# Loading one expert's second weight matrix whole instead of in column slabs, at the end of a soft-MoE kernel

## The chip, the cores and the metric

The kernel runs on one core of a Trainium2 chip. The metric is the device time of one execution in microseconds (us), lower is better. Every number below comes from the profiles, the traces or the timed runs of this kernel and its variants, except where the Trainium skill is named. Most executions of the kernel before agree within 0.3%. One run of the kernel before took 372.67 us and is left out wherever fast runs are compared.

In the profiles PE is TensorE's matmuls and PEld its weight loads, ACT is ScalarE, DVE is VectorE, POOL is GpSimd, SP is SyncE, which issues the stores. The granted clock (PEclk) is the share of TensorE's full clock that it was given. SBUF is the on-chip memory of tiles, PSUM the one in which the matmuls' sums lie, in parts called banks.

## The reference

Sliding-window and dilated attention (8 batches, 8 heads, 576 positions, 64 per head), followed by a soft mixture of experts (MoE). Only the second part matters here:

```python
logits = x @ phi                       # x: 4608 tokens x 512; phi: 512 x 32 slots
d = softmax(logits, axis=0)            # over tokens
slot_input = (d.T @ x).reshape(8, 4, 512)
for e in range(8):                     # w1[e]: 512 x 1024, w2[e]: 1024 x 512
    h = np.maximum(slot_input[e] @ w1[e], 0.0)
    slot_out[e] = h @ w2[e]            # 4 slots of each expert
out = softmax(logits, axis=1) @ slot_out.reshape(32, 512)   # 4608 x 512
```

No output row can be finished before all eight `w2` have arrived. But an output *column* needs only that column of every `w2`.

## The kernel before

A small list scheduler written in Python orders the instructions of all engines and adds the semaphore waits. Weights are read as 4-byte floats and written to SBUF as bf16 by DMAs issued from GpSimd, in one long stream behind q, k and v. The stream ends with `w2` of experts 6 and 7, and these two are loaded in two slabs of 256 columns: all of slab 0, then all of slab 1. While slab 1 is still coming in, the outputs of columns 0 to 255 are computed, and those of the first `NA = 2.5` groups of 512 tokens are stored by halves, in pieces of 256 KB. The other groups are stored with all 512 columns.

```python
wq += [w1_piece(e, 2 if e == 0 else 0) for e in range(8)]
wq += [w2_piece(e) for e in range(5)] + [w2_piece(5, 0, 4), w2_piece(5, 4, 4)]   # 5 in two halves by rows
for s in range(2):                                                               # 6 and 7 in slabs of columns
    wq += [w2_slab(6, s), w2_slab(7, s, 0, 4), w2_slab(7, s, 4, 2),
           w2_slab(7, s, 6, 1), w2_slab(7, s, 7, 1)]
# ... (cut)
l2((0, 1, 2, 3), 0, 0, 512)            # l2: the sum h @ w2 of these experts, rows 32*(e % 4) of a PSUM bank
l2((4,), 0, 0, 512)
for y in range(2):
    l2((5,), 0, 0, 512, range(4 * y, 4 * y + 4), [b_w5h[y]])
# SOx: ScalarE copies rows 0-63 (experts 0, 1, 4, 5: finished) to SBUF as bf16
# SOy: VectorE copies rows 64-127 (experts 2, 3) to SBUF as f32
for x in (1, 2):                       # column halves
    l2((6,), x, 256 * x - 256, 256, bufs=[b_w2[6][x - 1]])
    for y, cs in enumerate((range(4), range(4, 6), range(6, 7), range(7, 8))):
        l2((7,), x, 256 * x - 256, 256, cs, [b_w2h[y][x - 1]])
    # SO0, SO1: VectorE adds rows 64-127 of this bank (experts 6, 7) to the copy SOy
# ... (cut) output tiles of 128 tokens: one matmul, then ScalarE and VectorE in turn scale it into SBUF, then a store
```

PE waits at each `l2` until that piece of weights has landed (0.85 us before slab 0 of expert 6 in the trace below). And SO0 needs SOy, which needs everything summed into the bank before it.

The softmax here doesn't subtract the row's maximum and nothing guards it: scores larger than these inputs give would overflow.

## Time and profile before

| | before |
|---|---|
| median of the runs, us | 178.0 (3 runs), 177.87 (6 runs) |
| span of the profiled execution, us | 176.1 |
| last weight piece landed | 152.19 |
| first store issued | 148.57 |
| first store landed on all 16 engines | 152.90 |
| last store landed | 175.61 |

"Landed" is the last of the 16 semaphore increments of a transfer in the trace.

Four rows of the slice table of the profile page (kernel before). Each of the 40 digits is one slice of 4.4 us: busy share of PE in tenths, granted TensorE clock in tenths, busy share of the DMA engines, and GB/s written by them.

```profile
PE   0008786799698998999998989996779676797000
...
PEclk9999999789999999999999999999755999999955
DMA  5999999999999999999999999999999999999997
GB/s 186 233 210 210 224 201 210 227 201 209 220 210 208 219 214 208 214 217 205 216 215 204 209 216 221 220 212 216 216 220 203 204 195 196 296 312 415 422 419 318
```

DMA is busy all the time, so the time is that of the transfers: 61.9 MB read, then 9.44 MB stored. The table counts a load by what it writes as bf16, half of what it reads, so 216 GB/s there is some 430 GB/s of reading. The rise at slice 34 (from 149.7 us) is the first stores.

The transfers by issue (kernel before): KB as written, median us from issue to landing.

```profile
out_dram<-ar SPq DMA_DIRECT2D x6, 1024.0 KB, 8.6
...
ar<-in_moe_w_dram POOLq DMA_DIRECT2D x5, 512.0 KB, 28.1
out_dram<-ar SPq DMA_DIRECT2D x10, 256.0 KB, 3.8
```

The ten stores of 256 KB are the halves of two and a half groups.

The chain of waits that ended last, in order of time (kernel before): start, us, what.

```profile
120.13 32.05 DMA ar<-in_moe_w_dram
...
152.23 0.30 PE ps L857
...
152.55 0.44 DVE ar L881
...
153.04 0.42 PE ps L901 x2
```

From 120 to 152.19 us the chain is one wait for weights. After the last landing comes 0.3 us of matmul, one addition of 0.44 us, and outputs.

### The profile page before, as it was taken

What the parts mean: (1) busy time and instruction counts of PE and PEld (TensorE: products, weight loads), DVE (VectorE), ACT (ScalarE), POOL (GpSimd) and SP (SyncE); (2) the same over time, 40 slices, a digit from 0 to 9 for tenths busy, and PEclk for the clock granted to TensorE, in tenths of its full rate; (3) what the DMA queues carried; (4) which work ended last, traced back from release to release, by engine and by line L of the source; (5) the groups of instructions that cost most, each with busy time, mean ns of one, the idle gap of its engine ahead of it and who ended that gap; (6) DMA issues with size and microseconds to landing.
All of it is one profiled execution on the core that took longest, in us unless ns stands there. A gap on an engine that the chain in (4) does not pass through costs nothing.

```text
span 176.1 us, 4787 instructions
## 1 busy us (share of the span) xinstructions
PE 129.5 (74%) x2102; PEld 86.8 (49%) x2102; DVE 120.5 (68%) x218; ACT 104.4 (59%) x165; POOL 44.9 (25%) x90
## 2 busy tenths in 40 slices
PE   0008786799698998999998989996779676797000
PEld 0005564567566776676777567765434334431000
DVE  6899395669998989989998999657220014399200
ACT  2404378568879969889889788884301113299000
POOL 7659622214142223311460000394000000000000
PEclk9999999789999999999999999999755999999955
DMA  5999999999999999999999999999999999999997
GB/s 186 233 210 210 224 201 210 227 201 209 220 210 208 219 214 208 214 217 205 216 215 204 209 216 221 220 212 216 216 220 203 204 195 196 296 312 415 422 419 318
DMA packets 17492, 41.26 MB, mean 234 GB/s; under 512 B 1728, under 2 KB 8384, under 8 KB 15040
## 3 DMA queue, kind: packets, MB, share of 16 engines
q0 software_dynamic: 13328, 30.41, 90.2%
q1 hardware_dynamic: 4144, 10.55, 15.7%
q8 instruction: 16, 0.26, 0.5%
q14 instruction: 4, 0.03, 0.0%
HBM read 61.93 MB, written 9.44 MB: 405 GB/s over the span
## 4 chain that ended last, share of the span: by engine, by line
DMA 32%; PE 23%; DVE 21%; ACT 10%; POOL 4%; issue 2%; POOLq 0%; DVEq 0%
DMA ar<-in_moe_w_dram 18%; DMA ar<-in_v_dram 14%; PE ps L509 6%; DVE ar L488 6%; DVE ar L913 6%; ACT ar L548 5%; POOL ar L372 3%; PE ps L603 3%; PE ps L570 3%; ACT ar L670 2%; PE ps L693 2%; DVE ar L614 2%; PE ps L516 2%; PE ps L526 2%; ACT ar L576 2%
## 5 line engine op out<-in xcount | busy, mean ns | idle before, releaser
L548 ACT ACTIVATE ar<-ps 128x1152 bf16<-128x1152 f32 (+1 forms) x32 | 38.0, 1186 | 22.8 <-PE ps L533 13.2
L488 DVE STREAM_TRANSPOSE ar<-ar 128x576 uint32<-128x576 uint32 x40 | 48.3, 1239 | 0.6 <-DMA ar<-in_k_dram 0.3
L509 PE MATMUL ps<-ar 128*128 128x320 bf16 (+1 forms) x128 | 23.8, 312 | 15.5 <-DVE ar L488 13.7
L614 DVE TENSOR_TENSOR ar<-ps,fs 96x768 bf16<-96x768 f32 (+1 forms) x32 | 26.3, 822 | 1.2
L576 ACT ACTIVATE ar<-ps 128x768 bf16<-128x768 bf16 x32 | 25.0, 812 | 1.1 <-PE ps L570 1.0
L509 PEld LDWEIGHTS ps<-ar 128*128 128x128 bf16 x128 | 10.8, 102 | 21.0 <-DVE ar L488 13.7
L603 PE MATMUL ps<-ar 128*128 128x65 bf16 x320 | 15.6, 199 | 4.2 <-ACT ar L548 4.2
L570 PE MATMUL ps<-ar 128*128 128x128 bf16 x192 | 15.9, 229 | 1.8 <-DVE ar L614 1.0
L603 PEld LDWEIGHTS ps<-ar 128*128 128x128 bf16 x320 | 12.8, 101 | 7.4 <-ACT ar L548 4.8
L910 ACT ACTIVATE ar<-ps,fs 128x512 f32<-128x512 f32 (+1 forms) x23 | 11.4, 638 | 7.6 <-PE ps L901 7.6
L335 POOL DMA_DIRECT2D ar<-in_k_dram x16 | 8.9, 553 | 27.5 <-DVE ar L488 26.7
L610 DVE RECIPROCAL fs<-ps 96x12 f32<-96x12 f32 (+1 forms) x32 | 6.6, 206 | 12.7 <-PE ps L603 12.2
L570 PEld LDWEIGHTS ps<-ar 128*128 128x128 bf16 x192 | 12.4, 118 | 2.9 <-DVE ar L614 1.2
L913 DVE TENSOR_SCALAR ar<-ps,fs 128x512 f32<-128x512 f32 (+1 forms) x23 | 12.7, 629 | 1.0 <-PE ps L901 1.0
L335 POOL DMA_DIRECT2D ar<-in_v_dram x16 | 8.8, 547 | 13.7 <-DVE ar L488 10.4
L857 PE MATMUL ps<-ar 128*32 128x512 bf16 (+1 forms) x80 | 9.6, 338 | 2.9 <-DMA ar<-in_moe_w_dram 1.4
L693 PE MATMUL ps<-ar 128*128 128x288 bf16 x64 | 10.2, 307 | 1.2 <-ACT ar L677 1.2
L335 POOL DMA_DIRECT2D ar<-in_q_dram x16 | 8.7, 545 | 8.8 <-DVE fs L610 5.3
L901 PE MATMUL ps<-ar 128*128 128x512 bf16 (+1 forms) x46 | 9.9, 340 | 1.3 <-DVE ar L881 1.0
L670 ACT ACTIVATE ar<-ps 128x576 bf16<-128x576 bf16 x16 | 9.7, 659 | 0.9 <-PE ps L654 0.7
L673 ACT ACTIVATE ar<-ps 128x1024 bf16<-128x1024 bf16 x8 | 8.2, 1030 | 2.5 <-PE ps L660 2.3
L494 DVE STREAM_TRANSPOSE ar<-ar 128x160 uint32<-128x160 uint32 (+1 forms) x32 | 9.5, 409 | 0.1
(75 smaller groups left out, 182.8 us busy)
## 6 DMA issues: line engine op xcount, KB each, us to landing
ar<-in_moe_w_dram POOLq DMA_DIRECT2D x12, 1024.0 KB, 25.9
out_dram<-ar SPq DMA_DIRECT2D x6, 1024.0 KB, 8.6
ar<-in_k_dram POOLq DMA_DIRECT2D x16, 288.0 KB, 21.1
ar<-in_q_dram POOLq DMA_DIRECT2D x16, 288.0 KB, 21.5
ar<-in_v_dram POOLq DMA_DIRECT2D x16, 288.0 KB, 20.5
ar<-in_moe_w_dram POOLq DMA_DIRECT2D x5, 512.0 KB, 28.1
out_dram<-ar SPq DMA_DIRECT2D x10, 256.0 KB, 3.8
ar<-in_moe_w_dram SPq DMA_DIRECT2D x1, 1024.0 KB, 5.1
```

The costliest lines, as they stand in the source:

```text
L335: return pool.dma_start(a(o_stg + (s * 3 + j) * 1152, [[1, 1152]]), src[b, 4 * dl:4 * dl + 4].rearrange("h (p t) d -> (h p) (t d)", p=32))
L488: return dve.transpose(au(o_dst, [[1, 18], [18, 32]]), au(src, [[32, 18], [1, 32]]))
L509: pe.matmul(pf(h, 0, [[1, W]]), a(o_id, [[1, 128]]), a(msk, [[1, W]]), start=True, stop=False)
L548: eo = op(ACT, lambda P=P, W=W: act.activation(a(P, [[W, 4], [1, W]]), AP(ps, 0, [[4096, 128], [512, 4], [1, W]]), ACTF.Exp, scale=SCALE), ...
L570: last = pe.transpose(pb(bank.idx, bb * 256 + par * 32, [[64, 4], [1, 32]]), src, a(o_id, [[1, 128]]))
L576: op(ACT, lambda t=t, bank=bank: act.activation(a(o_vb[vs] + 3 * t * VBK, [[66, 12], [2, 32], [1, 2]]), pb(bank.idx, 0, [[64, 12], [1, 32] ...
L603: last = pe.matmul(pf(bank.idx + x, 65 * t, [[1, 65]]), w, a(VB + t * VBK + 66 * h, [[1, 65]]), start=True, stop=True)
L614: op(DVE, lambda hp=hp, bank=bank: dve.tensor_tensor(a(ox + 128 * hp, [[64, 2], [256, NT], [1, 64]], 0, rows), pf(bank.idx, 0, [[512, 2], ...
L670: fn = lambda c=c + x, bank=bank: act.activation(a(o_xt[xt] + 576 * c, [[1, 576]]), pb(bank.idx, 0, [[1, 576]]), ACTF.Copy)
L693: last = pe.matmul(pf(bank.idx, 0, [[1, 288]]), a(o_phis + 128 * c, [[1, 128]]), a(o_xt[xt] + 576 * c + 288 * g, [[1, 288]]), start=(c == ...
L910: op(ACT, lambda: act.activation(dst, src(), ACTF.Copy, scale=sca), actt(cw, .1), prio + .1, reads=[bank, b_rinv], writes=wr, name=f"OE{G} ...
L913: op(DVE, lambda: dve.tensor_scalar(dst, src(), sca, None, op0=AluOp.mult), dvet(cw, True) + .08, prio + .1, reads=[bank, b_rinv], writes= ...
```

## The change

Slabs of columns mean short packets: a slab is written in pieces of 512 B, a whole `w2` in pieces of 8 KB. The change keeps slabs for expert 7 alone, loads experts 5 and 6 whole, and stores two groups by halves instead of two and a half, since less of the stream is left to overlap with.

```diff
-    wq += [w2_piece(e) for e in range(5)] + [w2_piece(5, 0, 4), w2_piece(5, 4, 4)]
+    wq += [w2_piece(e) for e in range(7)]
     for s in range(2):
-        wq += [w2_slab(6, s), w2_slab(7, s, 0, 4), w2_slab(7, s, 4, 2),
+        wq += [w2_slab(7, s, 0, 4), w2_slab(7, s, 4, 2),
                w2_slab(7, s, 6, 1), w2_slab(7, s, 7, 1)]
# ... (cut: buffers, stop flags)
-    for y in range(2):
-        l2((5,), 0, 0, 512, range(4 * y, 4 * y + 4), [b_w5h[y]])
-    op(ACT, ... SOx: rows 0 to 63 ...)
-    op(DVE, ... SOy: rows 64 to 127 ...)
+    l2((5,), 0, 0, 512)
+    l2((6,), 0, 0, 512)
+    op(ACT, ... SOx: rows 0 to 95 ...)
+    op(DVE, ... SOy: rows 96 to 127 ...)
     for x in (1, 2):
-        l2((6,), x, 256 * x - 256, 256, bufs=[b_w2[6][x - 1]])
         for y, cs in enumerate((range(4), range(4, 6), range(6, 7), range(7, 8))):
             l2((7,), x, 256 * x - 256, 256, cs, [b_w2h[y][x - 1]])
-        op(DVE, ... SO0, SO1: rows 64 to 127 ...)
+        op(DVE, ... SO0, SO1: rows 96 to 127 ...)
-    NA = 2.5
+    NA = 2
```

Expert 6's sum, once two column halves behind their own slabs, becomes eight matmuls of 512 columns behind one landing, and SOx and SOy now come after them.

## The prediction

> **What bounds the kernel now.** The DMA engines, almost from end to end. The slice table has DMA at 9 tenths in every slice but the first and last, PE only 74% busy. In the chain of waits, the weight loads hold 120.1 to 152.2 us; evictions and stores follow. Two floors in a row: the load stream (61.9 MB read), whose last piece lands at 152.2 us (semaphore landings), and 9.44 MB of stores, last landed at 175.6 us.
>
> Packet records give the rates: whole-w2 loads (8 KB packets written) 429 GB/s of fp32 read; slabs of 256 columns (512 B packets) 388; half-width stores (1 KB rows) about 350, one 256 KB store every 0.75 us; full stores (8 KB) 420, 2.50 us per 1 MB. That short packets are slower agrees with the Trainium skill, "DMA: Bandwidth & Descriptors", section "Why small descriptors are slow". Loads and stores share the 16 engines (same page, "Issuing engines are not separate DMA queues"): from 149 to 152 us stores take 64, 172, 252 GB/s while slabs fall to 308, 198, 112. But the slabs are not delayed: their 2 MB took 5.43 us beside stores and 5.38 us without. Half of the engines finish each load some 2.3 us early, and the first stores fill these.
>
> **What changes, with costs (estimates from these durations).**
> 1. Expert 6's w2, 2.1 MB, at 429 instead of 388 GB/s: stream 0.5 us shorter, last landing 152.2 -> 151.7. Gain: 0.5 us. Expert 5 whole: nothing, 4 and 8 KB packets ran equally fast.
> 2. One half-width pair and a 512 KB store become part of a full store: 10 x 0.75 + 1.35 + 6 x 2.5 = 23.8 us becomes 8 x 0.75 + 7 x 2.5 = 23.5 us. Gain 0.3 us, partly hidden before in the early engines.
> 3. Loss: the first column half is complete later. After expert 5 came 5.4 us of slabs until 146.8 us; now 4.9 us (expert 6) + 2.7 us (expert 7's first slab): 149.0 us. The first store's issue moves from 148.6 to 150.8, its first bytes from 149.5 to 151.7 us, when the stream has ended on all engines: the early ones idle from 149.3, the late ones 0.3 us. The overlap is lost.
> 4. Expert 6's eight 512-column matmuls, 0.215 us each, finish at about 148.0 us, before the slabs need PE. The second half's first store can start its bytes 2.8 us after the last landing, at 154.5; four half stores cover 151.7 to 154.7. So no second hole, where before the early engines had one (258 and 187 GB/s at 153 to 155 us).
>
> **Sum.** First store lands at 152.8 to 152.9 (as before, 152.9), then 7 x 0.75 + 7 x 2.5 = 22.75 us: last landing about 175.6 us, against 175.6. The shorter stream pays for the stores' later start. Predicted time 177.9 us, 80% range 177.2 to 178.7. Faster by over 2%: 1%; within 2%: 97%; slower by over 2%: 2%.
>
> **What would show it.** (1) Last weight landing at 151.7, 0.5 us sooner. (2) First store issued near 150.8, with a dip in DMA in the slice at 149 to 152 us, and the dip at 153 to 155 gone. (3) 512 B packets halved, to 2048; 8 half stores. (4) All the same up to 136 us. (5) First store landed near 152.9, then stores back to back.
>
> **What would make it wrong.** A hole after the fourth half store (up to +0.7 us), if evictions or the last sum run late; a larger skew of the engines with 2 MB pieces; half stores at 0.68 us, as on the late engines before (-0.5 us).

## More of the kernel before

The clock is down in slices 28 to 30 (counted from 0), at half from 125.6 to 135.8 us in the trace, and full from there to 166 us.

The instructions between the end of expert 5 and the first store (timeline, kernel before): start, us, engine, line, what, and in brackets the idle time before and what ended it. L857 is `l2`, L872 and L875 are SOx and SOy, L881 is SO0, L901 the output matmuls.

```profile
143.27 0.59 ACT L872 ACTIVATE ar<-ps 64x512 bf16<-64x512 f32 x1 [5.84 <-PE ps L857]
143.27 0.69 DVE L875 COPY ar<-ps 64x512 f32<-64x512 f32 x1 [4.68 <-PE ps L857]
...
144.09 1.05 PE L857 MATMUL ps<-ar 128*32 128x256 bf16 x8 [0.85 <-DMA ar<-in_moe_w_dram]
...
145.47 1.61 PE L857 MATMUL ps<-ar 128*32 128x256 bf16 x8 [0.34 <-DMA ar<-in_moe_w_dram]
...
147.12 0.43 DVE L881 TENSOR_TENSOR ar<-ps,ar 64x256 bf16<-64x256 f32 x1 [3.16 <-PE ps L857]
...
147.61 1.29 PE L901 MATMUL ps<-ar 128*128 128x256 bf16 x10 [0.52 <-DVE ar L881]
147.94 1.93 ACT L910 ACTIVATE ar<-ps,fs 128x256 f32<-128x256 f32 x5 [4.08 <-PE ps L901]
...
148.57 2.86 SPq L922 DMA_DIRECT2D out_dram<-ar  x5
```

A group is shown with the shape of its first matmul, and a group of `l2` can hold several. The copies SOx and SOy are done at 143.96 us, long before slab 0 is complete at 146.76. What counts is therefore short: landing, the last matmul, SO0 at 147.12, output matmuls, evictions, first store issued at 148.57.

The same stretch by windows (kernel before): length in us, busy us of each engine with instruction counts, then granted clock, DMA share (the packets' times over the span of 16 engines, which comes out above 1 here), GB/s.

```profile
core 0: us, PE busy (x) PEld busy (x) DVE busy (x) ACT busy (x) POOL busy (x), PEclk, DMA share, GB/s
136.00:142.00 6.00, 4.67 (x68) 2.39 (x57) 0.36 (x2) 0.69 (x1) 0.00 (x0) 1.00 1.18 201
142.00:146.40 4.40, 3.18 (x22) 1.49 (x18) 0.69 (x1) 0.59 (x1) 0.00 (x0) 1.00 1.45 196
146.40:149.80 3.40, 2.20 (x16) 1.49 (x16) 2.17 (x6) 1.85 (x5) 0.00 (x0) 1.00 1.42 199
149.80:152.00 2.20, 1.90 (x14) 0.93 (x12) 0.31 (x1) 0.08 (x1) 0.00 (x0) 1.00 1.22 287
```

PE holds its full clock (1.00) all through.

## The result, and the profile after

The changed kernel ran at 179.46 us (median of 6, 178.84 to 180.1), outside the predicted 177.2 to 178.7. The ratio to before is 1.009, 95% interval 1.0066 to 1.0113. Ratios are the mean time of one kernel's fast runs over that of the other's of the same rounds, so they are not quite the ratio of the medians quoted. That is slower, but by less than 2%.

| | before | after | predicted |
|---|---|---|---|
| median, us | 177.87 | 179.46 | 177.9 |
| slab 0 landed | 146.76 | 149.11 | 149.0 |
| last weight landed | 152.19 | 151.82 | 151.7 |
| SOx and SOy start | 143.27 | 149.78 | not given; expert 6's sum ends at about 148.0 |
| first store issued | 148.57 | 152.08 | 150.8 |
| first store landed | 152.90 | 154.27 | 152.8 to 152.9 |
| last store landed | 175.61 | 177.18 | about 175.6 |

The slice table (kernel after; slices of 4.4 us):

```profile
PE   0009776799698999999999788995777457896000
...
PEclk9999999789999999999999999999999956999755
DMA  5999999999999999999999999999999999599997
GB/s 190 230 211 207 224 203 210 224 204 209 222 207 210 222 206 209 219 208 211 220 208 213 207 222 215 220 216 212 216 216 218 210 196 148 189 371 413 419 417 321
```

There is a DMA hole that was not there before: slices 33 and 34 (146.5 to 155.4 us) move 148 and 189 GB/s, against 196 and 296. And the clock row has moved: nothing at slices 28 to 30, but 5 and 6 in slices 32 and 33, just where expert 6 is summed.

The transfers by issue (kernel after):

```profile
ar<-in_moe_w_dram POOLq DMA_DIRECT2D x14, 1024.0 KB, 27.3
out_dram<-ar SPq DMA_DIRECT2D x7, 1024.0 KB, 8.6
...
out_dram<-ar SPq DMA_DIRECT2D x8, 256.0 KB, 2.8
```

The transfers are as intended.

The chain of waits (kernel after):

```profile
114.13 32.27 DMA ar<-in_moe_w_dram
...
146.44 3.31 PE ps L856 x12
...
149.78 0.71 DVE ar L874
...
150.58 0.44 DVE ar L879
...
151.15 0.40 PE ps L899 x2
...
151.57 1.66 DVE ar L911 x4
```

The chain no longer hangs on the last weights. It leaves the weights at 146.40 us, with expert 6's landing, and then runs through 3.31 us of matmuls, the copy SOy (0.71), the addition SO0 and the first evictions.

The timeline from expert 6's landing to the first store (kernel after; L856 is `l2`, L871 and L874 are SOx and SOy, L879 is SO0, L899 the output matmuls):

```profile
146.44 3.30 PE L856 MATMUL ps<-ar 128*32 128x512 bf16 x16 [2.15 <-DMA ar<-in_moe_w_dram]
...
149.78 0.59 ACT L871 ACTIVATE ar<-ps 96x512 bf16<-96x512 f32 x1 [15.35 <-PE ps L856]
149.78 0.70 DVE L874 COPY ar<-ps 32x512 f32<-32x512 f32 x1 [14.19 <-PE ps L856]
150.58 0.43 DVE L879 TENSOR_TENSOR ar<-ps,ar 32x256 bf16<-32x256 f32 x1
...
151.15 1.04 PE L899 MATMUL ps<-ar 128*128 128x256 bf16 x8 [1.41 <-DVE ar L879]
151.46 1.20 ACT L908 ACTIVATE ar<-ps,fs 128x256 f32<-128x256 f32 x3 [1.09 <-PE ps L899]
151.57 0.88 DVE L911 TENSOR_SCALAR ar<-ps,fs 128x256 f32<-128x256 f32 x2 [0.57 <-PE ps L899]
152.08 0.39 SPq L920 DMA_DIRECT2D out_dram<-ar  x1
```

The first line holds sixteen matmuls: the eight of expert 6 (512 columns, rows 64 to 95) and, from 148.13 us beside them, the eight of slab 0 of expert 7 (256 columns, rows 96 to 127). The eight matmuls of expert 6 begin 0.43 us apart; expert 5's, before, began 0.215 us apart with the same 512 columns. They end at 149.74 us. SOy ends at 150.48, and SO0 starts 3.5 us later than before, where the landing of slab 0 was only 2.35 us later.

The same windows as before (kernel after):

```profile
136.00:142.00 6.00, 3.71 (x42) 1.53 (x31) 0.00 (x0) 0.00 (x0) 0.00 (x0) 1.00 1.03 216
142.00:146.40 4.40, 2.30 (x7) 0.60 (x5) 0.00 (x0) 0.00 (x0) 0.00 (x0) 0.55 1.14 195
146.40:149.80 3.40, 3.30 (x16) 1.62 (x16) 0.02 (x1) 0.02 (x1) 0.00 (x0) 0.57 1.28 171
149.80:152.00 2.20, 0.85 (x8) 0.80 (x8) 1.53 (x4) 1.11 (x3) 0.00 (x0) 1.00 0.42 56
```

The granted clock is 0.55 and 0.57 in the two windows from 142.0 to 149.8. In the trace the clock is at half from 142.5 to 149.3 us.

### The profile page after: what moved, and what is told of

The parts are those of the page before. It is cut to its first block, busy times and chain, and to the rows that moved or that the text cites. A ratio compares the mean times of both kernels' runs of the same rounds, so it can differ in the third digit from the quotient of the medians.

```text
span 177.6 us, 4758 instructions
## 1 busy us (share of the span) xinstructions
PE 126.3 (71%) x2092; PEld 85.5 (48%) x2092; DVE 120.3 (68%) x217; ACT 104.2 (59%) x164; POOL 43.0 (24%) x88
## 4 chain that ended last, share of the span: by engine, by line
DMA 32%; PE 24%; DVE 23%; ACT 10%; issue 2%; DVEq 0%; POOL 0%
DMA ar<-in_moe_w_dram 18%; DMA ar<-in_v_dram 14%; DVE ar L911 7%; PE ps L508 6%; DVE ar L487 6%; ACT ar L547 5%; PE ps L602 3%; PE ps L569 3%; ACT ar L669 2%; PE ps L692 2%; DVE ar L613 2%; PE ps L515 2%; PE ps L856 2%; PE ps L525 2%; ACT ar L575 2%
## 5 line engine op out<-in xcount | busy, mean ns | idle before, releaser
L856 PE MATMUL ps<-ar 128*32 128x512 bf16 (+1 forms) x72 | 10.7, 404 | 4.9 <-DMA ar<-in_moe_w_dram 4.4
L899 PE MATMUL ps<-ar 128*128 128x512 bf16 (+1 forms) x44 | 9.9, 347 | 2.3 <-DVE ar L879 2.0
L874 DVE COPY ar<-ps 32x512 f32<-32x512 f32 x1 | 0.7, 696 | 14.2 <-PE ps L856 14.2
L856 PEld LDWEIGHTS ps<-ar 128*32 128x32 bf16 x72 | 4.7, 107 | 10.7 <-DMA ar<-in_moe_w_dram 5.8
```

What stands on the lines that cost most here:

```text
L856: last = pe.matmul(pf(sobank[x].idx, 0, [[1, n]], 32 * j, 32), a(o_htz + 1024 * g + 128 * c + 32 * j, [[1, 32]]), a(w2off(e) + DM * c + co ...
```

## The experiments

Three theories were set against each other.

- **A, the clock.** With whole pieces PE waits longer between pieces, falls to half clock, and the sum of expert 6 takes 3.3 us instead of 1.7. SOy stands behind it, so the first store goes out 1.3 us late.
- **B, the order of the loads.** Slab 0 lands 2.35 us later, whatever PE does, and that alone costs the time.
- **C, the stores.** Two groups by halves cover too little.

Fillers below are matmuls whose results nobody reads. They are put where PE would wait for weights, and write rows that expert 7's first matmul clears, or, in the second dose, rows that nothing reads. A rival outside the three, that the scheduler reorders other work, is ruled out by the traces: after with its variants warm, soyearly and dose_same_rows, and before with before_fill_b, have the same order of instructions on ACT, DVE and SP, and on PE apart from the edit. All variants gave correct results. Each was timed in five rounds beside the kernel before.

### Fillers that keep PE busy (warm)

```diff
     l2((4,), 0, 0, 512)
+    fill(10, "4")       # ten matmuls of 512 columns on weights that are there
     l2((5,), 0, 0, 512)
+    fill(10, "5")
     l2((6,), 0, 0, 512)
```

> The changed kernel with ten filler matmuls (512 columns, result never read) after the sum of expert 4 and ten after that of expert 5, while PE waits for weights. Same loads, stores and copies. Theory A (half clock: expert 6's eight matmuls took 3.3 us instead of 1.7, so the first store was issued at 152.1 instead of 150.8): PE stays at full clock after 136 us, the eight matmuls end near 148.2, the first store is issued near 150.9, the last store lands near 175.8, and the time is 178.0 us, 0.8% under the changed kernel, although work was added. Rival B (the first column half simply lands later, 149.1 instead of 146.8, whatever PE does) and rival C (fewer half stores to overlap with): unchanged, 179.4 us.

Measured: 178.2 us, ratio 1.0009 (0.9995 to 1.0023). SOx and SOy started at 148.14, the first store was issued at 150.68, the last landed at 175.77. Windows of the variant with fillers:

```profile
142.00:146.40 4.40, 3.43 (x24) 1.47 (x23) 0.00 (x0) 0.00 (x0) 0.00 (x0) 1.00 1.13 193
146.40:149.80 3.40, 2.71 (x17) 1.19 (x16) 1.13 (x2) 0.59 (x1) 0.00 (x0) 1.00 1.29 172
```

PE has more to do (3.43 us instead of 2.30 in the first of these windows) and the clock is 1.00. Twenty matmuls more make the kernel 0.8% faster (1.009 against 1.0009, each to the kernel before). B and C, which expected no effect, cannot be the cause of these 0.8%.

### Experts 5 and 6 in halves by rows (halves)

```diff
-    wq += [w2_piece(e) for e in range(7)]
+    wq += [w2_piece(e) for e in range(5)] + [w2_piece(e, c0, 4) for e in (5, 6) for c0 in (0, 4)]
-    l2((5,), 0, 0, 512)
-    l2((6,), 0, 0, 512)
+    for e in (5, 6):
+        for y in range(2):
+            l2((e,), 0, 0, 512, range(4 * y, 4 * y + 4), [b_w6h[e - 5][y]])
```

> The changed kernel with w2 of experts 5 and 6 each loaded in two halves by rows (4 KB packets, as fast as 8 KB ones), each with its own four matmuls. Slabs and stores as in the changed kernel. Theory A: only four matmuls are left after the last landing at 146.4, and PE has work every 2.45 us, so that the clock need not fall; end of expert 6 at 147.4 (full clock) to 148.2 (half), first store issued near 150.9, 178.0 us. Rivals B and C: the first slab lands at 149.1 all the same and the stores are the same, 179.4 us.

Measured: 178.56 us, ratio 1.0028 (1.0014 to 1.0041). SOx and SOy started at 148.29, first store issued at 151.23. The clock fell all the same, from 146.2 to 149.6 us, so that slab 0's last sums ran at half clock and SO0 started at 149.71. About two thirds of the loss are gone, which fits the little work that is left after the landing. The guess that the clock would hold was wrong in this profile.

### The copy SOy ahead of expert 6 (soyearly)

```diff
     l2((5,), 0, 0, 512)
+    op(DVE, ... SOy ...)     # rows 96 to 127 hold experts 3 and 7 only, and 7 is in another bank
     l2((6,), 0, 0, 512)
-    op(DVE, ... SOy ...)
```

> The changed kernel with the copy of rows 96 to 127 to SBUF (0.70 us on VectorE, which stood between expert 6's last matmul at 149.75 and the addition at 150.58) moved ahead of expert 6: those rows hold experts 3 and 7 only. Theory A, in which the chain goes through expert 6's slow matmuls: the addition starts near 149.85, ScalarE's copy of 0.6 us is next and ends at 150.4, the first output matmul at 150.45 instead of 151.15, first store issued near 151.4, 178.8 us if the clock is half as before. Rivals B and C: 179.4 us.

Measured: 178.79 us, ratio 1.0042 (1.0028 to 1.0055). The clock was at half from 146.5 to 149.9 us, SOx started at 149.97, first store issued at 151.65. So the copy was a real link of the chain behind a late sum: 0.43 us of first store in these profiles, where 0.7 had been hoped for. The sum itself ended 0.19 us later here.

### The stores of the change alone (stores_only)

```diff
 # in the kernel before
-    NA = 2.5
+    NA = 2
```

> The kernel before with only the stores of the change: two groups by halves instead of two and a half; loads and sums as before. Rival C (too few half stores): 1 us or more slower than before, 178.9 to 179.5. Theory A: the late engines are free some 0.3 us before the second column half can be stored, then 3 x 0.75 + 7 x 2.5 us follow: 0.2 to 0.5 us over before, 178.1 to 178.4; first store issued at 148.6 as before.

Measured: 178.25 us, ratio 1.0016 (1.0002 to 1.0029). C fails, since it asked for 178.9 or more. The profile of this variant holds more than was asked for. Its windows:

```profile
146.40:149.80 3.40, 2.72 (x14) 1.36 (x12) 1.65 (x4) 1.44 (x4) 0.00 (x0) 0.50 1.37 185
149.80:152.00 2.20, 2.20 (x15) 1.64 (x15) 0.54 (x2) 0.32 (x1) 0.00 (x0) 0.50 1.14 266
```

Here PE happened to be at half clock while slabs 6 and 7 were summed (145.4 to 152.2 us in the trace), and it hardly mattered: the first store was issued at 149.16, 0.6 us later than in the kernel before. With small pieces, each summed as it lands, a slow PE has little left to do after the last one.

### A measured dose of delay at full clock (dose_b, dose_same_rows)

A first submission of this and the next three found no chip. They were sent again, hence the ending of the labels.

```diff
 # in the variant with fillers
     fill(10, "5")
+    fill(8, "5", 6)     # eight matmuls that wait for expert 6's weights: 8 x 0.215 us
     l2((6,), 0, 0, 512)
```

> The run with fillers that kept PE at full clock, plus eight more filler matmuls (512 columns, 0.215 us each at full clock) between expert 6's landing and its sum: the delay of the half clock, 1.7 us, put back at full clock as work. Theory A (what counts is how long PE needs after expert 6 has landed at 146.2): expert 6's sum ends near 149.7, first store issued near 152.1, time 179.4 to 179.8, as the changed kernel. If the fillers had helped in some other way than through the clock and the length of that sum: 178.2.

Measured: 178.91 us, ratio 1.0056 (1.0044 to 1.0068), below what was expected. Expert 6's matmuls write rows 64 to 95, the fillers rows 96 to 127. The trace shows the two running beside each other: expert 6's first started at 147.31 us, the last filler at 147.96. The delay added to SOx was 1.11 us, not 1.7 (149.25 against 148.14). So the dose was repeated with fillers on rows 64 to 95:

> The earlier dose was half a microsecond too small: its eight fillers wrote output rows 96 to 127 and expert 6's matmuls, which write rows 64 to 95, ran partly beside them (first at 147.31, while fillers ran to 148.2). Here the fillers write rows 64 to 95, so that they cannot overlap. Theory A: expert 6's sum ends a full 16 x 0.215 us after 146.4, at 149.9, then 0.70 us of copy and 0.43 us of addition: first store issued at 152.1 to 152.3, last store landed 25.1 us after that, 177.2 to 177.4; time 179.4 to 179.6. If the delay does not go through this sum: 178.9 as with the other dose.

Measured: 179.84 us, ratio 1.0114 (1.0101 to 1.0127). SOx started at 150.02, SOy 0.01 later, the first store was issued at 152.40, the last landed at 177.51. Its windows:

```profile
142.00:146.40 4.40, 3.48 (x25) 1.49 (x24) 0.00 (x0) 0.00 (x0) 0.00 (x0) 1.00 1.10 188
146.40:149.80 3.40, 3.40 (x24) 1.85 (x24) 0.00 (x0) 0.00 (x0) 0.00 (x0) 1.00 1.31 175
```

At full clock, the same length of work behind expert 6's landing brings the whole loss back, and 0.2 to 0.4 us more than expected. It is the length of that sum which costs. The clock is one way to make it long.

### The loads of the change alone (loads_only_b)

```diff
 # in the changed kernel
-    NA = 2
+    NA = 2.5
```

> The change without its stores: whole w2 of experts 5 and 6, slabs of 7 only, but still two and a half groups stored by halves. Theory A: PE falls to half clock in the same place and the first store is issued near 151.7 to 152.1; two more half stores cost 2 x 0.75 + 1.35 - 2.5 = 0.35 us: 179.3 to 179.9. Rival C (the loss is the shorter cover by half stores): about as before, 178.0.

Measured: 179.87 us (178.6 to 180.76), ratio 1.0097 (1.0065 to 1.013). Half clock from 142.8 to 149.6, first store issued at 152.33. The times make two groups here, too: four from 179.83 to 180.76, two at 178.6. With stores_only, this puts the loss on the loads and the sums behind them.

### Control: fillers in the kernel before (before_fill_b)

```diff
 # in the kernel before
     l2((4,), 0, 0, 512)
+    fill(5, "4")
     for y in range(2):
         l2((5,), 0, 0, 512, range(4 * y, 4 * y + 4), [b_w5h[y]])
+        fill(5, "5")
```

> Control: fifteen filler matmuls in the kernel before, around the two halves of expert 5. In its profile PE was at full clock from 135.8 us on, so that there is nothing to win: 177.8 to 178.2, ratio 0.999 to 1.001; first store issued at 148.6. If fillers help by themselves: about 177.2.

Measured: 177.92 us, ratio 1.0002 (0.999 to 1.0015). First store issued at 148.82. In this profile, in which the clock was full from 17 to 164 us, the fillers gained nothing: PE's work was not what the first store waited for.

### Everything together (warm_halves_early_b)

Fillers, experts 5 and 6 in halves, and the early SOy in the changed kernel.

> The changed kernel with everything that takes work out of the stretch after expert 6's landing: fillers, experts 5 and 6 in halves by rows, and the early copy. Theory A: nothing is left but the landing of the first slab at 149.0, first store issued at 150.6 to 150.7, last store landed at 175.7, 178.0 to 178.2: no better than fillers alone (ratio 1.001 to before) and not better than before, because the stores' later start eats the 0.5 us of the shorter stream.

Measured: 178.29 us, ratio 1.0023 (1.0011 to 1.0035). SOx started at 147.50, first store issued at 150.97, last landed at 176.08. Nothing is left between the landing of slab 0 (149.10) and SO0 (149.46) but the last matmul. So theory B holds for the remainder: the late landing of slab 0 eats the 0.4 to 0.6 us by which the stream got shorter. No version tried here beats the kernel before.

### The changed kernel once more (after_again)

> The changed kernel once more, for its spread on the same chip as the dose. Theory A (the half clock falls on expert 6's sum in nearly every run, but its phase against the kernel differs): median 179.2 to 179.7 with a spread of 1 us or more, while kernels kept at full clock spread 0.3 to 0.6 us; the first store is issued 25.1 us before the last landing.

Measured on the chip of the second dose: 179.42, 179.25, 178.21, 178.31, 179.54 and 178.26 us, median 178.78, ratio 1.0045 (1.0021 to 1.0068). The median fell below what was expected. The times make two groups, three around 178.26 and three around 179.40. The profiled one (179.42) belongs to the slow group; its clock was at half from 146.4 to 149.9 us and its first store was issued at 152.02. The fast group is where the variant with fillers was (178.2). The runs without a trace at hand list only the mean clock of the whole execution, which does not tell the groups apart (0.929 to 0.960 against 0.921 to 0.949). That the fast ones had full clock at expert 6 fits all the rest, but is not shown. The three fast runs lie inside the range that had been predicted: whether a single run agrees with the prediction is, on this account, a matter of luck with the clock.

### Expert 5 whole in the kernel before (before_w5whole)

```diff
 # in the kernel before
-    ... + [w2_piece(5, 0, 4), w2_piece(5, 4, 4)]
+    ... + [w2_piece(5)]
-    for y in range(2):
-        l2((5,), 0, 0, 512, range(4 * y, 4 * y + 4), [b_w5h[y]])
+    l2((5,), 0, 0, 512)
```

> The kernel before with only expert 5 loaded whole and summed in one go, slabs of 6 and 7 as before. The prediction called this free. Theory A: PE waits longer and may fall to half clock here too, but after it come the small slab sums, of which only 0.2 to 0.5 us is left after the last landing: first store issued at 148.6 to 149.2 and 177.8 to 178.3. If the whole piece of expert 5 is itself what costs: 179 or more.

Measured: 177.94 us, ratio 0.9999 (0.9987 to 1.0011). PE waited longer for expert 5 and the clock fell to half from 141.7 to 145.2 us, which the first line shows as 0.64 (windows of this variant):

```profile
142.00:146.40 4.40, 4.38 (x21) 2.09 (x19) 0.69 (x1) 0.59 (x1) 0.00 (x0) 0.64 1.45 195
146.40:149.80 3.40, 2.22 (x16) 1.40 (x15) 2.06 (x6) 1.74 (x5) 0.00 (x0) 1.00 1.39 191
```

SOx started 1.75 us later than before (145.02), and still 1.85 us before slab 0 was complete (146.87), so the first store went out at 148.75. The slack behind expert 5 took it all.

### The runs side by side

| | clock over 146.4 to 149.8 | SOx starts | first store issued | last store landed | last landing minus first issue | median, us | ratio |
|---|---|---|---|---|---|---|---|
| before | 1.00 | 143.27 | 148.57 | 175.61 | 27.04 | 177.87 | |
| changed | 0.57 | 149.78 | 152.08 | 177.18 | 25.10 | 179.46 | 1.0090 |
| changed, again | 0.51 | 149.71 | 152.02 | 177.17 | 25.15 | 178.78 | 1.0045 |
| warm | 1.00 | 148.14 | 150.68 | 175.77 | 25.09 | 178.20 | 1.0009 |
| halves | 0.53 | 148.29 | 151.23 | 176.32 | 25.09 | 178.56 | 1.0028 |
| soyearly | 0.51 | 149.97 | 151.65 | 176.72 | 25.07 | 178.79 | 1.0042 |
| dose_b | 1.00 | 149.25 | 151.63 | 176.74 | 25.11 | 178.91 | 1.0056 |
| dose_same_rows | 1.00 | 150.02 | 152.40 | 177.51 | 25.11 | 179.84 | 1.0114 |
| warm_halves_early_b | 1.00 | 147.50 | 150.97 | 176.08 | 25.11 | 178.29 | 1.0023 |

In every variant with the loads and stores of the change, the last store lands 25.1 us after the first one is issued. From there on nothing but DMA counts, so each tenth of a microsecond on the way to the first store is paid in full. In the kernel before the number is 27.04, because its first stores begin while the stream still runs. It starts them 3.5 us earlier and ends only 1.6 us earlier.

## Why the prediction was wrong

**What held.** The stream became shorter (last landing 151.82, predicted 151.7). Slab 0 landed at 149.11 (149.0). Loading expert 5 whole cost nothing in the kernel before (before_w5whole); its share in the changed kernel was not measured alone. There was no second hole: the DMA engines moved 320 GB/s or more from 153 us on. Eight half stores and seven full ones followed each other without a gap, at 0.78 us (0.75 predicted) and 2.50 us (2.50). The claim that the shorter stream just pays for the later start of the stores was right for a PE at full clock: the variant with fillers has ratio 1.0009.

**The step that failed.** "Expert 6's eight 512-column matmuls, 0.215 us each, finish at about 148.0 us, before the slabs need PE." The 0.215 us had been read from the trace of before, in a stretch at full clock, and used for a stretch where the change itself alters how busy PE is. In the profiled run of after they began 0.43 us apart and finished at 149.74, 0.63 us after slab 0 had landed (149.11). SOy, which the prediction left out, came after them and held up SO0 until 150.58. The first store was issued at 152.08, not 150.8.

**The sum mended.** The first store landed at 154.27 instead of 152.85, 1.42 us late; the half stores took 7 x 0.776 = 5.43 us instead of 5.25; the full ones 17.48 instead of 17.5. That is 177.18 us, 1.6 more than predicted. Of the 1.42 us, 1.28 are in the first store's issue and 0.14 between issue and landing (2.19 us, where the prediction allowed 2.05). Of the 1.28, 1.11 are SO0's wait for the late sum and the copy SOy behind it: SO0 would have started near 149.47, 0.36 us after slab 0's landing as in the kernel before. Slab 0 landing later than worked out is 0.11. The variant with fillers takes the delay of 1.11 us away (SO0 0.36 us after slab 0), and the dose at full clock puts it back.

**Why the clock fell.** The trace gives the times at which the granted clock changes, and they lie on a grid of 3.41 us whose phase against the kernel differs from run to run. The Trainium skill, "TensorE: Matmul & The Clock Gate", section "Part 1: The HAM clock gate", says that the clock is set by how busy PE was in a free-running window of that length. The trace agrees with the length: in after the clock fell at the end of the window 139.1 to 142.5 us, in which matmuls covered 1.12 us (the end of expert 4, then a wait of 2.3 us for expert 5). It came back at the end of 145.9 to 149.3. In before, the windows over the same stretch held 2.2 us or more. Over the 13 profiles, from 36 to 165 us, take the time that matmul records cover in each window of the grid that began at full clock: every window with 1.57 us or less lost the full clock, windows with 1.60 to 1.79 us did so in seven of twelve cases, and none with 1.87 us or more did. The way back is another matter: of the windows at half clock, some with up to 3.2 us of matmul records stayed there.

The comparison of these two traces alone would mislead. In before, PE was at half clock until 135.8 us and began the sums at 138.74 us, three microseconds later than in after (135.6), so it had less to wait for. But in after_again PE was at half clock until 136.2 us, too, and lost the full clock again at 146.4: the window 143.0 to 146.4, with the wait for expert 6, held 0.58 us of matmuls, while the nearest one in before (142.7 to 146.1, with small pieces) held 2.2. So the larger pieces came with longer waits, and then a burst at half clock. They are not the only way to it: in stores_only, with the small pieces, the clock fell at 145.4 us.

**Why before does not suffer.** Its variants with the slabs of expert 6 did meet half clock near the same place (stores_only, before_w5whole) and lost little or nothing. The kernel before sums each small piece as it lands, and its copies are done 2.8 us ahead of need. The change puts eight long matmuls and a copy between a landing and the first store. That removed the slack, and the clock then became visible.

**What stays open.** Which single runs of the changed kernel fell into half clock is not known for those without a trace, so how often it happens is only inferred from the two groups of times. The size of the loss depends on it: the ratio was 1.009 in the first session and 1.0045 in the second. One execution of the fast group with its trace would settle it.

## What to carry to other kernels

A duration read from a trace holds for the clock at which it was read: when a change makes PE wait longer between bursts, work out the burst after the wait at half clock as well, and check whether its end is then on the chain. Near the end of a load stream, what counts is how much work stands between the last landing that gates the first store and that store; small pieces that are summed as they land, and copies taken as early as their rows are final, protect it. A shorter stream is no gain if the first store starts later by as much.

## What the Trainium skill lacked or had wrong

- "TensorE: Matmul & The Clock Gate", section "Part 1: The HAM clock gate", has the half clock begin after at least one idle window of some 3.4 us. Here PE need not be idle: of the windows that began at full clock, those with up to 1.57 us of matmuls in 3.41 us always lost it, those with 1.60 to 1.79 us sometimes, those with 1.87 us or more never (13 profiles).
- The same section puts the penalty of warming up below 1% of a typical span. The size agrees: changed kernels at half clock took about 1.3 us, 0.7 to 0.8%, longer than the variant with fillers. What the section does not say is that the cost of one such stretch depends on the chain: here it decided the case, because the way to the first store ran through the half-clock stretch, and where there was slack a half clock of 3.4 us cost nothing (before_w5whole, 177.94 us).
- "DMA: Bandwidth & Descriptors", section "Latency and other measured facts", names two of the 16 engines as usually slower. In the slab loads of the kernel before, half of the 16 landing increments came some 2 us after the other half (last slab piece: eight from 149.59 to 150.52 us, eight from 151.49 to 152.19).
- The same page has no rates on trn2 for loads that convert 4-byte floats to bf16: here 429 GB/s of reading with 8 KB packets written and 388 with 512 B packets; nor for stores of 1 KB rows, about 350 GB/s, against 420 with 8 KB.
